# Attention over channels and a feed-forward layer in one kernel: the first pair of chunks by eight plain products, sums of the first weights later, other places for the first loads

## The chip, the cores and the metric

The kernel runs on one core of a Trainium2 chip. The metric is the device time of one execution in microseconds (us); of the kernel before there are three runs. One further execution was recorded by the profiler. Its page calls the engines PE (matrix engine; PEld is its loading of the stationary operand), DVE (vector engine), ACT (scalar engine), POOL and SP (which issues the transfers).

## The reference

For each of 4 batches with N = 6080 tokens and C = 256 channels, k and q are normalised along the tokens, a 256 x 256 score matrix of channel against channel goes through a softmax, and v is multiplied by it. The result goes through a feed-forward layer of width 2048 with the exact gelu.

```
qn = q / (norm(q, axis=1) + 1e-06);  kn = k / (norm(k, axis=1) + 1e-06)
s = kn.transpose(0, 2, 1) @ qn / tau
a = exp(s - s.max(-1));  a /= a.sum(-1) + 1e-09
x = (v @ a).reshape(B * N, C)
h = x @ w_in
out = (0.5 * h * (1 + erf(h / sqrt(2)))) @ w_out
```

The feed-forward weights come as float64.

## The kernel before, in words

The attention matrix is folded into the first weights. For each batch the kernel computes a @ w_in (256 x 2048, in four groups of 512 columns, `w_group`), so that tokens go straight from v to h. All large products are done in three passes on pairs (high, low) of a rounded value and its remainder: high x high, high x low, low x high.

**Opening.** `load_first` loads 24 tiles of 512 KB with q and k of batch 0, then the first four of batch 1 (`FILL`), 13 tiles ahead (`AHEAD`). `qk_first` adds each tile to the scores. The squares for the norms come from two sources: for the first `NSQ` tiles from the tiles themselves (`squares`: a square on ACT, an add on DVE), for the rest from a transposed copy of q and k in pieces of 512 KB (`norm_part`, squares with a sum on ACT). Between the tiles there are loads of v for the first pair (`load_v`, 1 MB) and of the first units of raw weights. `qk_fill` gives PE score matmuls of batch 1 during the softmax of batch 0.

**Narrowing.** The float64 weights are turned into high and low parts on the chip, 16 units of 512 columns: `narrow` is eight DVE operations and two on ACT, in an order where most wait for the one before. Units "in" feed `w_group`, units "out" feed the second products. `load_w` puts a raw unit in one of three buffers (`raw`), so the load of a later unit waits until an earlier one is narrowed; two of the units use buffers of their own (`raw_w`). `NARROWS` says behind which score tiles a unit is narrowed, `paces` how many behind each step of the first pair. The narrowed parts are also stored to DRAM (`keep`), from where later pairs load them.

**Main part.** Tokens are taken in pairs of chunks of up to 512 (`PAIRS`, six per batch) and hidden columns in eight units of 256 (`NU`), so a step is (batch, pair, unit). `first_products` computes the 2 x 2 blocks of h with Strassen's seven products (Winograd's form), 21 matmuls. It needs sums of the weight blocks (S1 to S4) and of the v blocks (T1 to T4), copies three partial results on ACT (L461) and adds on DVE (L466), then takes gelu twice on ACT (L449 and L450) and its remainder on DVE (L451). `second_products`, 24 matmuls (L511 to L513), runs one step behind, interleaved with the first products of the next step. `extras` issues what lies beside a step: the next weight group at the first pair's units 0, 2 and 4, loads, sums for the next pair. `w_group` has 12 matmuls (L362 to L364), and the weights' sums and splits follow it at once; for the very first group they are taken in the order in which the products need them (`w_split`).

**Order.** Dependencies are tracked by tile. A planner places the instructions on each engine by its own estimates of times, with a priority by the order of the text; the softmax and the first weight group have a higher one. On the chip each engine then keeps that order, so a PE matmul at the head of the queue whose input is late holds up what stands behind it. Buffers are shared by name: a new tile of a name waits until the old one's last reader is done.

```
ORDER = ((A11, B11), (S1, T1), (S2, T2), (A12, B21), (S3, T3), (S4, B22), (A22, T4))
```

Of the kernel before, what the change touches and what calls it, by code (L numbers as in the profile page):

```python
# [10 lines left out]
F32R = mybir.dt.float32r  # L11
U32 = mybir.dt.uint32
# [4 lines left out]
P = 128  # L17
# [22 lines left out]
NSJ = NS // (JS * P)  # L40
NSC = NJ * P // NS

NSQ = 4 * NSJ

NARROWS = (4, 7, 12, 18, 20)

GAPS = (7, 4, 2)

# [2 lines left out]

A11, A22, A12, S1, S2, S3, S4 = range(7)
B11, B21, B22, T1, T2, T3, T4 = range(7)


@with_exitstack
def channel_attention_gelu_ffn(ctx, tc, qk, kqt, vt, tau, w_in, w_out, out):
# [30 lines left out]
    def f32(ap):  # L88
        return ap.bitcast(F32)
# [117 lines left out]

    def load_w(src):

        if len(units) in (11, 12):  # L210
            raw = pst.tile([P, src.shape[-1], 2], U32, name="raw_w", bufs=2)
        else:
            raw = pqk.tile([P, src.shape[-1], 2], U32, name="raw", bufs=3)
        nc.sync.dma_start(out=raw, in_=src.bitcast(U32).rearrange("p (n w) -> p n w", w=2))
        return raw

# [126 lines left out]
        state["e"], state["rden"] = (eh, el), rden  # L343


    def w_split(g, i, src):
        nc.scalar.copy(out=whs[g][:, i], in_=src)
        nc.vector.tensor_tensor(out=wls[g][:, i], in0=src, in1=f32(whs[g][:, i]), op=ALU.subtract)  # L348

    def w_group(b, g):  # L350

        eh, el = state["e"]
        win = wins.pop((b, g))
        first = (b, g) == (0, 0)
        tmp = pqk.tile([P, 8, 2, P], F32, name="hl")
        a21, a11, a22, a12 = (tmp[:, i] for i in range(4))
        s1, s2, s3, s4 = (tmp[:, 4 + i] for i in range(4))
        for m in range(NCT):
            cs = slice(m * P, (m + 1) * P)
            pwt = bank()  # L360
            for d in range(NCT):
                nc.tensor.matmul(pwt, eh[:, d, cs], win[:, 0, d], start=(d == 0), stop=False)  # L362
                nc.tensor.matmul(pwt, eh[:, d, cs], win[:, 1, d], start=False, stop=False)
                nc.tensor.matmul(pwt, el[:, d, cs], win[:, 0, d], start=False, stop=(d == NCT - 1))  # L364
            nc.scalar.activation(out=tmp[:, 2 * m:2 * m + 2], in_=pwt.rearrange("p (q r c) -> p r q c", q=2, r=2),
                                 func=AF.Copy, scale=state["rden"][:, m:m + 1])
            if first and m == 0:
                w_split(g, A11, a11)
        tt = nc.vector.tensor_tensor
        if first:  # L370

            tt(out=s1, in0=a21, in1=a22, op=ALU.add)
            w_split(g, S1, s1)
            tt(out=s2, in0=s1, in1=a11, op=ALU.subtract)
            w_split(g, S2, s2)
            w_split(g, A12, a12)
            tt(out=s3, in0=a11, in1=a21, op=ALU.subtract)
            w_split(g, S3, s3)
            tt(out=s4, in0=a12, in1=s2, op=ALU.subtract)
            w_split(g, S4, s4)  # L380
            w_split(g, A22, a22)
            return
        tt(out=s1, in0=a21, in1=a22, op=ALU.add)
        tt(out=s3, in0=a11, in1=a21, op=ALU.subtract)
        tt(out=s2, in0=s1, in1=a11, op=ALU.subtract)
        tt(out=s4, in0=a12, in1=s2, op=ALU.subtract)
        for to, of in ((slice(0, 3), slice(1, 4)), (slice(3, 7), slice(4, 8))):
            (nc.scalar.copy if b == 0 else nc.vector.tensor_copy)(out=whs[g][:, to], in_=tmp[:, of])
            tt(out=wls[g][:, to], in0=tmp[:, of], in1=f32(whs[g][:, to]), op=ALU.subtract)


# [2 lines left out]
    def load_v(b, p):  # L394
        t0, n = PAIRS[p]
        raw = pv.tile([P, NCT, 2 * NT], F32, name="v_raw")
        nc.sync.dma_start(out=raw[:, :, :2 * n],
                          in_=vt[:, b * N + t0:b * N + t0 + 2 * n].rearrange("(t p) n -> p t n", p=P))
        vraw[b, p] = raw
# [20 lines left out]
    def v_split(b, p, i):  # L420
        n = PAIRS[p][1]
        x = v_blocks(b, p)
        src = {B11: x[0, 0], B21: x[1, 0], B22: x[1, 1]}.get(i)
        if src is None:
            src = vts[b, p][i - T1][:, :n]
        hi = pv.tile([P, NT], F32R, name=f"vh{i}")
        lo = pv.tile([P, NT], F32R, name=f"vl{i}")
        nc.scalar.copy(out=hi[:, :n], in_=src)
        nc.vector.tensor_tensor(out=lo[:, :n], in0=src, in1=f32(hi[:, :n]), op=ALU.subtract)
        vops[b, p, i] = hi, lo  # L430
# [23 lines left out]
    def first_products(b, p, u):  # L454
# [38 lines left out]
        do(6, one, False, True)  # L493
        out[0, 0] = gelu(one[:, :n], n)

    po = {}

    def second_products(b, p, u, blocks):
# [32 lines left out]
    def load_unit():  # L531
        kind, g, d = units.pop(0)
        src = w_in64[:, d, g * NT:(g + 1) * NT] if kind == "in" else w_out64[:, g * 2 * C:(g + 1) * 2 * C]
        loaded.append((kind, g, d, load_w(src)))
# [28 lines left out]
             ("in", 2, 0), ("in", 2, 1), ("out", 2, 0), ("out", 3, 0), ("in", 3, 0), ("in", 3, 1), ("out", 4, 0),  # L563
             ("out", 5, 0), ("out", 6, 0), ("out", 7, 0)]

    paces = (1, 2, 1, 2, 2, 1, 1)
    loaded = deque()


    pieces = [(t, c) for c in range(NSQ // NSJ, NSC) for t in range(2 * NCT)]  # L570
    for i in range(AHEAD):
        load_first(i)
        if i in (1, 3, 9):
            load_unit()
        if i in (5, 8, 11):
            norm_part(0, *pieces.pop(0))
        if i == 7:
            load_v(0, 0)
    nc.sync.dma_start(out=taut, in_=tau)
    nc.vector.reciprocal(out=rtau, in_=taut)  # L580
    for js in range(NQS):
        qk_first(js)
        if js + AHEAD < NQS + FILL:
            load_first(js + AHEAD)
            if js % 2 == 1 and pieces:
                norm_part(0, *pieces.pop(0))
        elif len(units) > 11:
            load_unit()
        if js in NARROWS:
            narrow_unit()  # L590
        if js in (10, 11):
            v_sums(0, 0, js - 10)
        if 12 <= js < 19:
            v_split(0, 0, ORDER[js - 12][1])
    for x in held:
        keep(*x)
    fill = qk_fill()
# [29 lines left out]
    def extras(b, p, u):  # L627

        w = p * NU + u
        nxt = (b, p, u + 3)  # L630
        if nxt[2] >= NU:
            nxt = (b, p + 1, nxt[2] - NU)
        if nxt[1] == NP:
            nxt = (b + 1, 0, nxt[2])
        if nxt[0] < B and nxt[:2] != (0, 0):
            load_wo(nxt)
        if (b, p) == (0, 0):
            if u % 2 == 0 and u // 2 + 1 < NWG:
                w_group(0, u // 2 + 1)
        if b > 0 and w == 1:  # L640
            w_group(b, NWG - 1)
        pair = (b, p + 1) if p + 1 < NP else (b + 1, 0)
        if pair[0] < B:
            if u == 1:
                load_v(*pair)
            if u in (4, 5):
                v_sums(*pair, u - 4)
        if b + 1 == B:
            return
        start, num, den = (8, 5, 2) if b == 0 else (2, 3, 1)  # L650
        for k in range(FILL // NB if b == 0 else 0, NQS // NB):
            at = start + k * num // den
            if w == at:
                for m in range(NCT):
                    burst(b + 1, k, m)
                for t in range(NB):
                    hls.pop((b + 1, k * NB + t))
            before = start + (k - 1) * num // den
            if w == (before + 1 if k else at - 1):
                for t in range(NB):  # L660
                    split_qk(b + 1, k * NB + t)
            if w == (before if k else at - 2):
                for t in range(NB):
                    load_qk(b + 1, k * NB + t)
        n0 = 8
        if n0 <= w < n0 + 2 * NCT * NSC:
            with behind("kept"):
                norm_part(b + 1, *divmod(w - n0, NSC))
        if w == 37:
            state["stages"] = softmax(False, ps_h, "ph")  # L670
        if w >= 37:
            next(state["stages"], None)
        if w in (40, 42, 44, 46):
            load_win(b + 1, (w - 40) // 2)
        if w in (42, 44, 46):
            w_group(b + 1, (w - 42) // 2)
# [2 lines left out]
    second = iter(())  # L679
    for b, p, u in steps:  # L680
        pair = (b, p + 1) if p + 1 < NP else (b + 1, 0)
        for i, _ in enumerate(first_products(b, p, u)):
            next(second, None)
            if u == NU - 1 and pair[0] < B:
                v_split(*pair, ORDER[i][1])
        if u == NU - 1 and pair[0] < B:
            v_split(*pair, ORDER[6][1])
        for _ in second:
            pass
        if (b, p) == (0, 0):  # L690
            for _ in range(paces[u] if u < len(paces) else 0):
                narrow_unit()
                if units:
                    load_unit()
        extras(b, p, u)
        second = second_products(b, p, u, state.pop("blocks"))
# [30 lines left out]
```

## Time and profile before

| | |
|---|---|
| time, median of 3 runs | 2208.83 us (2208.10 to 2211.41) |
| span of the profiled execution (its own time) | 2207.9 us |
| PE busy | 2179.6 us (99%) |
| DVE busy | 1402.2 us (64%) |
| ACT busy | 1444.0 us (65%) |
| DMA, mean over the span | 122 GB/s |

A busy share is an average over stages. The opening lasts to about 55 us, softmax and first weights to about 69, the first pair to about 180; there other engines are fuller than the average. In rows of instructions the figures are start (or none, in groups), time, engine, line of the kernel, operation, written tile <- read tiles, shape and count; what stands in brackets is idle time of the engine before the instruction, and what ended it.

### The profile page before, as it was taken

Reading aid. Unit: us, or ns where it says so; the run is one execution under the profiler, and the core shown is the slowest. Engines: PE = TensorE matmul, PEld = TensorE weight load, DVE = VectorE, ACT = ScalarE, POOL = GpSimd, SP = SyncE. Lnnn points to the kernel's source line nnn. Section 1 sums busy time; section 2 is a strip of 40 time slices with the busy share of each in tenths; the row PEclk is TensorE's granted clock in tenths of the full one; section 3 lists DMA queues with packets and bytes.
Section 4 is the critical chain, followed back from the end, with each engine's and each line's share of the span. In section 5 each row is a group of like instructions: output and inputs, shape, how many; then the busy total and the mean of one; then the engine's idle time right before and its main releaser. Section 6 shows DMA issues by size and latency. Waiting matters only on the chain.

```text
span 2207.9 us, 26235 instructions
## 1 busy us (share of the span) xinstructions
PE 2179.6 (99%) x9640; PEld 1787.3 (81%) x9640; DVE 1402.2 (64%) x2205; ACT 1444.0 (65%) x2625; POOL 1.3 (0%) x8
## 2 busy tenths in 40 slices
PE   8899999999999999999999999999999999999999
PEld 6678777888888888888888888888888888888888
DVE  6896757565576665756667657567466555554554
ACT  6678887557875565665766656656576666666665
POOL 0000000000000000000000000000000000000000
PEclk9999999999999999999999999999999999999999
DMA  9557775232652332322224223232122122222221
GB/s 377 196 170 253 243 238 190 78 112 89 235 192 84 125 105 86 109 93 91 89 103 143 98 85 124 67 124 95 48 105 93 59 89 71 70 87 69 73 76 48
DMA packets 77632, 269.61 MB, mean 122 GB/s; under 512 B 7744, under 2 KB 9792, under 8 KB 75456
## 3 DMA queue, kind: packets, MB, share of 16 engines
q1 hardware_dynamic: 77504, 267.94, 35.7%
q8 instruction: 76, 1.25, 0.2%
q14 instruction: 52, 0.43, 0.1%
HBM read 234.62 MB, written 33.29 MB: 121 GB/s over the span
## 4 chain that ended last, share of the span: by engine, by line
PE 87%; ACT 5%; DMA 4%; DVE 3%; issue 1%; SPq 0%; ACTq 0%; DVEq 0%
PE po L513 15%; PE po L511 14%; PE po L512 14%; PE ph L443 13%; PE ph L441 13%; PE ph L442 13%; DMA kqc<-kqt 3%; PE ph L187 2%; ACT kqc L205 2%; PE ph L189 1%; ACT gh L449 1%; ACT g L450 1%; DVE acc L135 1%; DMA raw<-qk 1%; DMA v_raw<-vt 1%
## 5 line engine op out<-in xcount | busy, mean ns | idle before, releaser
L451 DVE TENSOR_TENSOR gl<-g,gh 128x512 fp32r<-128x512 f32 (+1 forms) x768 | 522.6, 682 | 158.1 <-ACT g L450 155.9
L513 PE MATMUL po<-gh,wo 128*128 128x512 f32 (+1 forms) x1536 | 604.7, 394 | 0.0
L511 PE MATMUL po<-gh,wo 128*128 128x512 f32 (+1 forms) x1536 | 597.4, 390 | 0.0
L512 PE MATMUL po<-gl,wo 128*128 128x512 f32 (+1 forms) x1536 | 596.2, 388 | 0.5 <-DVE gl L451 0.5
L466 DVE TENSOR_TENSOR h<-ph,p 128x512 f32<-128x512 f32 (+1 forms) x384 | 262.5, 684 | 520.0 <-PE ph L443 406.1
L449 ACT ACTIVATE gh<-h 128x512 fp32r<-128x512 f32 (+1 forms) x576 | 360.9, 627 | 288.2 <-DVE h L466 284.5
L441 PE MATMUL ph<-vh,wh 128*128 128x512 f32 (+1 forms) x1344 | 526.1, 392 | 9.4 <-ACT p L461 4.0
L443 PE MATMUL ph<-vh,wl 128*128 128x512 f32 (+1 forms) x1344 | 526.5, 392 | 0.0
L442 PE MATMUL ph<-vl,wh 128*128 128x512 f32 (+1 forms) x1344 | 525.5, 391 | 0.0
L461 ACT COPY p<-ph 128x512 f32<-128x512 f32 (+1 forms) x384 | 221.9, 583 | 249.4 <-PE ph L443 249.1
L450 ACT ACTIVATE g<-h 128x512 f32<-128x512 f32 (+1 forms) x576 | 352.7, 612 | 0.0
L512 PEld LDWEIGHTS po<-gl,wo 128*128 128x128 f32 x1536 | 288.5, 188 | 64.9 <-DVE gl L451 1.2
L511 PEld LDWEIGHTS po<-gh,wo 128*128 128x128 f32 x1536 | 288.2, 188 | 62.4 <-ACT gh L449 1.5
L513 PEld LDWEIGHTS po<-gh,wo 128*128 128x128 f32 x1536 | 288.4, 188 | 61.5
L441 PEld LDWEIGHTS ph<-vh,wh 128*128 128x128 f32 x1344 | 252.9, 188 | 71.0 <-ACT p L461 8.4
L442 PEld LDWEIGHTS ph<-vl,wh 128*128 128x128 f32 x1344 | 253.2, 188 | 55.9
L443 PEld LDWEIGHTS ph<-vh,wl 128*128 128x128 f32 x1344 | 253.0, 188 | 51.8 <-DVE wl L348 0.2
L461 ACT COPY u<-ph 128x512 f32<-128x512 f32 (+1 forms) x192 | 111.7, 582 | 113.6 <-PE ph L443 113.5
L466 DVE TENSOR_TENSOR h<-ph,u 128x512 f32<-128x512 f32 (+1 forms) x192 | 131.1, 683 | 3.3
L450 ACT ACTIVATE g<-ph 128x512 f32<-128x512 f32 (+1 forms) x192 | 112.0, 583 | 0.0
L449 ACT ACTIVATE gh<-ph 128x512 fp32r<-128x512 f32 (+1 forms) x192 | 110.4, 575 | 0.0
L187 PE MATMUL ph<-hl 128*128 128x512 f32 x272 | 96.0, 392 | 0.0
(131 smaller groups left out, 1309.8 us busy)
## 6 DMA issues: line engine op xcount, KB each, us to landing
wo<-keep_out SPq DMA_DIRECT2D x184, 512.0 KB, 3.3
raw<-qk SPq DMA_DIRECT2D x95, 512.0 KB, 4.4
kqc<-kqt SPq DMA_DIRECT2D x72, 512.0 KB, 4.4
v_raw<-vt SPq DMA_DIRECT2D x20, 1024.0 KB, 5.2
out<-osb SPq DMA_DIRECT2D x40, 512.0 KB, 3.2
win<-keep_in SPq DMA_DIRECT2D x12, 1024.0 KB, 4.8
kq<-kqt SPq DMA_DIRECT2D x8, 512.0 KB, 9.0
raw<-w_out SPq DMA_DIRECT2D x8, 512.0 KB, 3.8
```

The costliest lines, as they stand in the source:

```text
L187: nc.tensor.matmul(s, hl[:, 0, j, 0, cs], hl[:, :, j, 1], start=(i == 0), stop=False, skip_group_check=True)
L441: nc.tensor.matmul(ps[:, :n], wh, hi[:, :n], start=start, stop=False, skip_group_check=True)
L442: nc.tensor.matmul(ps[:, :n], wh, lo[:, :n], start=False, stop=False, skip_group_check=True)
L443: nc.tensor.matmul(ps[:, :n], wl, hi[:, :n], start=False, stop=stop, skip_group_check=True)
L449: nc.scalar.activation(out=gh[:, :n], in_=src, func=AF.Gelu)
L450: nc.scalar.activation(out=g[:, :n], in_=src, func=AF.Gelu)
L451: nc.vector.tensor_tensor(out=gl[:, :n], in0=g[:, :n], in1=f32(gh[:, :n]), op=ALU.subtract)
L461: nc.scalar.copy(out=t[:, :n], in_=ps[:, :n])
L466: nc.vector.tensor_tensor(out=h[:, :n], in0=ps[:, :n], in1=t[:, :n], op=ALU.add)
L511: nc.tensor.matmul(o, wo[:, 0, i, cs], gh[:, :n], start=first, stop=False)
L512: nc.tensor.matmul(o, wo[:, 0, i, cs], gl[:, :n], start=False, stop=False)
L513: nc.tensor.matmul(o, wo[:, 1, i, cs], gh[:, :n], start=False, stop=last)
```

## The change

1. The first pair of chunks of the first batch is done by `plain_products`: four blocks of h, each the sum of two products in PSUM, 24 matmuls per unit in place of 21. No copies and no adds follow; gelu reads PSUM. Of v it needs the blocks B11, B21, B12, B22 and no sums; B12 uses T1's buffers. Of the weights it needs A11, A12, A21, A22 and no sums; A21 lies in buffers of T2 and T3.
2. In the first batch `w_group` splits these four blocks in `w_first`. The sums S1 to S4 and their splits, first used by the second pair, are in `w_sums`, called at units 0, 2, 4, 6 of the first pair.
3. `NSQ` goes from 16 to 20 tiles, so four norm pieces are left instead of eight.
4. Places of the first loads: weight units behind tiles 3, 10 and 27 (1, 3 and 9 before), norm pieces behind 7, 14, 17 and 20, v behind 25 (7 before). Two units are narrowed in the opening, behind tiles 12 and 18, in place of five; each step of the first pair narrows two. The buffers `raw_w` go.

As `plain_products` yields seven times, the last operand of the next pair is split twice in the last unit.

```
-NSQ = 4 * NSJ
-NARROWS = (4, 7, 12, 18, 20)
+NSQ = 5 * NSJ
+EXTRAS = {3: 'w', 7: 'n', 10: 'w', 14: 'n', 17: 'n', 20: 'n', 25: 'v', 27: 'w'}
+NARROWS = (12, 18)
...
+    def w_both(hi, lo, src):
+        nc.scalar.copy(out=hi, in_=src)
+        nc.vector.tensor_tensor(out=lo, in0=src, in1=f32(hi), op=ALU.subtract)
+    def w_first(g, m, tmp):
+        if m == 0:
+            name = (f"vh{T2}", f"vl{T2}", f"vh{T3}", f"vl{T3}")[g]
+            a21s[g] = pv.tile([P, 2, 2, P], F32R, name=name)
+            w_both(whs[g][:, A11], wls[g][:, A11], tmp[:, 1])
+            w_both(a21s[g][:, 0], a21s[g][:, 1], tmp[:, 0])
+        else:
+            w_both(whs[g][:, A12], wls[g][:, A12], tmp[:, 3])
+            w_both(whs[g][:, A22], wls[g][:, A22], tmp[:, 2])
+    def w_sums(g):
+        tmp = wtmp.pop(g)
+        a21, a11, a22, a12, s1, s2, s3, s4 = (tmp[:, i] for i in range(8))
+        tt = nc.vector.tensor_tensor
+        tt(out=s1, in0=a21, in1=a22, op=ALU.add)
+        tt(out=s3, in0=a11, in1=a21, op=ALU.subtract)
+        tt(out=s2, in0=s1, in1=a11, op=ALU.subtract)
+        tt(out=s4, in0=a12, in1=s2, op=ALU.subtract)
+        w_both(whs[g][:, S1:], wls[g][:, S1:], tmp[:, 4:])
...
+    def plain_products(b, p, u):
...
+        rows = {1: ((wh[:, A11, q], wl[:, A11, q]), (wh[:, A12, q], wl[:, A12, q])),
+                0: ((a21[:, 0, q], a21[:, 1, q]), (wh[:, A22, q], wl[:, A22, q]))}
+        cols = {0: (B11, B21), 1: (B12, B22)}
+        for j in range(2):
+            for i in (1, 0):
+                ps = bank()
+                for k in range(2):
+                    ah, al = rows[i][k]
+                    hi, lo = vops[b, p, cols[j][k]]
+                    for t, (x, y) in enumerate(((ah, hi), (ah, lo), (al, hi))):
+                        nc.tensor.matmul(ps[:, :n], x, y[:, :n], start=(k == 0 and t == 0),
+                                         stop=(k == 1 and t == 2), skip_group_check=True)
+                    if k == 0:
+                        yield
+                out[i, j] = gelu(ps[:, :n], n)
+                if (i, j) != (0, 1):
+                    yield
...
-    paces = (1, 2, 1, 2, 2, 1, 1)
+    paces = (2, 2, 2, 2, 2, 2, 1)
...
+            if u % 2 == 0:
+                w_sums(u // 2)
...
-        for i, _ in enumerate(first_products(b, p, u)):
+        plain = (b, p) == (0, 0)
+        for i, _ in enumerate((plain_products if plain else first_products)(b, p, u)):
```

More of the change, by code (lines that the diff above doesn't have):

```diff
@@ L53 @@
 B11, B21, B22, T1, T2, T3, T4 = range(7)
+B12 = T1
 @with_exitstack
@@ L208, in load_w @@
     def load_w(src):
[L210 to L213, printed above, removed]
+        raw = pqk.tile([P, src.shape[-1], 2], U32, name="raw", bufs=3)
         nc.sync.dma_start(out=raw, in_=src.bitcast(U32).rearrange("p (n w) -> p n w", w=2))
@@ L343, in softmax @@
         state["e"], state["rden"] = (eh, el), rden
-    def w_split(g, i, src):
-        nc.scalar.copy(out=whs[g][:, i], in_=src)
-        nc.vector.tensor_tensor(out=wls[g][:, i], in0=src, in1=f32(whs[g][:, i]), op=ALU.subtract)
+    a21s = {}
+    def w_both(hi, lo, src):
[19 more added lines that the diff above has]
+        w_both(whs[g][:, S1:], wls[g][:, S1:], tmp[:, 4:])
+    wtmp = {}
     def w_group(b, g):
@@ L353, in w_group @@
         win = wins.pop((b, g))
-        first = (b, g) == (0, 0)
         tmp = pqk.tile([P, 8, 2, P], F32, name="hl")
@@ L366, in w_group @@
                                  func=AF.Copy, scale=state["rden"][:, m:m + 1])
-            if first and m == 0:
-                w_split(g, A11, a11)
-        tt = nc.vector.tensor_tensor
[L370 to L382, printed above, removed]
+            if b == 0:
+                w_first(g, m, tmp)
+        if b == 0:
+            wtmp[g] = tmp
+            return
+        tt = nc.vector.tensor_tensor
         tt(out=s1, in0=a21, in1=a22, op=ALU.add)
@@ L387, in w_group @@
         for to, of in ((slice(0, 3), slice(1, 4)), (slice(3, 7), slice(4, 8))):
-            (nc.scalar.copy if b == 0 else nc.vector.tensor_copy)(out=whs[g][:, to], in_=tmp[:, of])
+            nc.vector.tensor_copy(out=whs[g][:, to], in_=tmp[:, of])
             tt(out=wls[g][:, to], in0=tmp[:, of], in1=f32(whs[g][:, to]), op=ALU.subtract)
@@ L423, in v_split @@
         src = {B11: x[0, 0], B21: x[1, 0], B22: x[1, 1]}.get(i)
+        if (b, p) == (0, 0) and i == B12:
+            src = x[0, 1]
         if src is None:
@@ L494, in first_products @@
         out[0, 0] = gelu(one[:, :n], n)
+    def plain_products(b, p, u):
+        n = PAIRS[p][1]
+        g, q = divmod(u, 2)
+        out = state["blocks"] = {}
+        wh, wl = whs[g], wls[g]
+        a21 = a21s[g]
+        rows = {1: ((wh[:, A11, q], wl[:, A11, q]), (wh[:, A12, q], wl[:, A12, q])),
[15 more added lines that the diff above has]
+                    yield
     po = {}
@@ L564, in channel_attention_gelu_ffn, with extra @@
              ("out", 5, 0), ("out", 6, 0), ("out", 7, 0)]
-    paces = (1, 2, 1, 2, 2, 1, 1)
+    paces = (2, 2, 2, 2, 2, 2, 1)
     loaded = deque()
     pieces = [(t, c) for c in range(NSQ // NSJ, NSC) for t in range(2 * NCT)]
+    def extra(i):
+        kind = EXTRAS.get(i)
+        if kind == "w":
+            load_unit()
+        elif kind == "n":
+            norm_part(0, *pieces.pop(0))
+        elif kind == "v":
+            load_v(0, 0)
     for i in range(AHEAD):
         load_first(i)
[L573 to L578, printed above, removed]
+        extra(i)
     nc.sync.dma_start(out=taut, in_=tau)
@@ L584, in channel_attention_gelu_ffn @@
             load_first(js + AHEAD)
-            if js % 2 == 1 and pieces:
-                norm_part(0, *pieces.pop(0))
+            extra(js + AHEAD)
         elif len(units) > 11:
@@ L590, in channel_attention_gelu_ffn @@
             narrow_unit()
[L591 to L594, printed above, removed]
+    for i in (B11, B21, B12, B22):
+        v_split(0, 0, i)
     for x in held:
```

## The prediction

> **What bounds the kernel now.** I read the page first, then windows of busy time, then what TensorE (PE) waited for, then the order of time around the longest waits.
>
> ```profile
> span 2207.9 us, 26235 instructions
> PE 2179.6 (99%) x9640; PEld 1787.3 (81%) x9640; DVE 1402.2 (64%) x2205; ACT 1444.0 (65%) x2625; POOL 1.3 (0%) x8
> ```
>
> The windows (length, then busy time and instructions of PE, PEld, DVE, ACT, POOL, then granted clock, DMA share, GB/s; DVE is VectorE, ACT is ScalarE):
>
> ```profile
> 46.00:62.50 16.50, 16.36 (x83) 13.80 (x83) 4.12 (x16) 6.35 (x14) 0.00 (x0) 1.00 1.02 397
> 62.50:176.00 113.50, 103.36 (x424) 79.20 (x424) 109.47 (x207) 80.97 (x152) 0.00 (x0) 0.97 0.49 171
> 68.58:176.00 107.42, 98.35 (x400) 75.33 (x401) 103.77 (x193) 75.34 (x141) 0.00 (x0) 0.97 0.46 158
> 88.00:118.00 30.00, 30.00 (x131) 24.11 (x130) 29.32 (x55) 21.74 (x39) 0.00 (x0) 1.00 0.34 119
> 140.00:176.00 36.00, 36.00 (x154) 28.36 (x155) 35.51 (x63) 27.40 (x52) 0.00 (x0) 1.00 0.55 188
> 76.20:83.10 6.90, 5.78 (x13) 4.10 (x14) 5.08 (x11) 4.96 (x9) 0.00 (x0) 0.51 0.37 152
> ```
>
> PE is busy for 99% of the span, so what counts is matmuls issued and time in which none starts. The change lies in the first 180 us. There, from 62.5 to 176, VectorE is busy 109.47 of 113.5 us: it is the full engine of that stretch, beside PE.
>
> PE's waits (in all, times, longest), first before 56 us, then from 68 to 190:
>
> ```profile
> PE ph L145 <- DMA raw<-qk: 7.7, 6, 3.5
> ```
>
> ```profile
> PE ph L363 <- DVE win L247: 4.2, 4, 2.0
> PE ph L362 <- ACT win L245: 2.1, 1, 2.1
> PE ph L441 <- ACT g L450: 1.3, 1, 1.3
> PE ph L441 <- ACT p L461: 1.2, 1, 1.2
> PE ph L441 <- ACT wh L347: 1.1, 1, 1.1
> PE ph L441 <- DVE h L466: 0.3, 1, 0.3
> ```
>
> And PE's pace in a full stretch:
>
> ```profile
> 101.40 0.39 PE L511 MATMUL po<-gh,wo 128*128 128x512 f32 x1
> ...
> 104.88 0.40 PE L513 MATMUL po<-gh,wo 128*128 128x512 f32 x1
> ```
>
> Sixteen matmuls start from 101.40 to 104.88, so one costs 3.48/15 = 0.232 us. Then 400 matmuls from 68.58 to 176 need 92.8 us and PE lost 107.4 - 92.8 = 14.6 us there. Saturated VectorE alone is not the loss: from 140 to 176 it is busy 35.51 of 36 and PE's 154 matmuls (35.7 us) fill the window; from 88 to 118 likewise. The loss sits where a matmul of the next weight group (L362, L363) stands at the head of PE's queue and its weights are still being narrowed:
>
> ```profile
> 68.58 0.50 PE L441 MATMUL ph<-vh,wh 128*128 128x512 f32 x1 [1.07 <-ACT wh L347]
> ...
> 70.83 0.40 PE L362 MATMUL ph<-win,eh 128*128 128x512 f32 x1
> 72.03 0.50 PE L363 MATMUL ph<-win,eh 128*128 128x512 f32 x1 [0.81 <-DVE win L247]
> 72.36 0.40 PE L364 MATMUL ph<-win,el 128*128 128x512 f32 x1
> 74.82 0.50 PE L362 MATMUL ph<-win,eh 128*128 128x512 f32 x1 [2.06 <-ACT win L245]
> 77.31 0.80 PE L363 MATMUL ph<-win,eh 128*128 128x512 f32 x1 [1.99 <-DVE win L247]
> ```
>
> and right after it, from 76.2 to 83.1, the granted clock is 0.51. The 13 matmuls there would take 3.0 us at the full pace; of the other 3.9, some 1.2 is the end of the last wait, so the slow clock cost about 2.7.
>
> **The change, part by part.** *First loads.* PE's matmuls on a tile of q and k are pitched like this, and loads follow each other on SP so:
>
> ```profile
> 8.34 1.99 PE L145 MATMUL ph<-raw 128*128 128x256 f32 x8 [1.01 <-DMA raw<-qk]
> ...
> 28.83 26.26 PE L145 MATMUL ph<-raw 128*128 128x256 f32 x112 [0.57 <-DMA raw<-qk]
> ```
>
> ```profile
> 12.16 0.34 SPq L119 DMA_DIRECT2D raw<-qk  x1
> 13.44 0.33 SPq L204 DMA_DIRECT2D kq<-kqt  x1
> ```
>
> The 112 matmuls of 14 tiles take 26.26 us, 1.88 a tile; a 512 KB load takes 13.44 - 12.16 = 1.28 us. Up to the last tile the queue now carries 24 tiles, 3 weight units, 8 norm pieces and v (two loads' worth): 37 x 1.28 = 47.4 us, more than PE's 24 x 1.88 = 45.1. After the change it is 24 tiles, 2 units and 4 pieces: 38.4. So the waits behind the first tile (7.7 - 3.5 = 4.2 us) have no cause; bounds 0 and 4.2, and I take 3.8, since the second tile (1.01) is early in the ramp. V moves from behind the 8th tile to behind the 26th: it is in after 34 loads, some 45 us, and its first use is the first product, now at 68.58; that gap is its cover. Four squares and four adds replace four squares over norm pieces; the adds, of 128x1024 (1.22 us each, L389 below), fall in VectorE's idle time, 12.4 of the 16.5 us from 46 to 62.5. Without that cover the last add would put 1.2 on the path.
>
> *Products.* A unit of the first pair goes from 21 to 24 matmuls: 8 x 3 x 0.232 = **+5.6 us** on PE, nothing hides it. The Trainium skill, page "TensorE: Matmul & The Clock Gate", section "Back-to-back issue gap", gives about 131 ns sustained for 512 columns; by it this term would be 3.1 us and the forecast 2.5 us lower. The row has 232 ns and decides. In return each unit sheds three copies on ScalarE and three adds on VectorE.
>
> ```profile
> 121.44 0.68 DVE L466 TENSOR_TENSOR h<-ph,u 128x512 f32<-128x512 f32 x1
> 122.04 0.68 DVE L451 TENSOR_TENSOR gl<-g,gh 128x512 fp32r<-128x512 f32 x1
> ```
>
> ```profile
> 126.05 0.42 DVE L235 TENSOR_SCALAR kqc<-raw 128x512 uint32<-128x512 uint32 x1
> 126.39 0.69 DVE L239 SCALAR_TENSOR_TENSOR kqc<-kqc,raw 128x512 f32<-128x512 f32 x1
> ```
>
> ```profile
> L389 DVE TENSOR_TENSOR wl<-hl,wh 128x1024 fp32r<-128x1024 f32 x3 | 3.7, 1218 | 0.0
> L389 DVE TENSOR_TENSOR wl<-hl,wh 128x768 fp32r<-128x768 f32 x3 | 2.8, 948 | 0.0
> ```
>
> ```profile
> L384 DVE TENSOR_TENSOR hl<-hl 128x256 f32<-128x256 f32 x3 | 1.3, 417 | 0.0
> ```
>
> In these pairs of rows, and the groups by shape, starts are 0.60 apart for a two-input 128x512 operation and 0.34 for a one-input one; a 128x256 sum lasts 0.42 and also gives 0.34. VectorE sheds 24 x 0.60 = 14.4 us.
>
> *Weights and narrowing.* One narrowing is three of 0.34 and five of 0.60 on VectorE: 4.0 us. Three leave the opening, but two of those (the raw_w ones) ran after 62.5 already, so the stretch gains one: +4.0. A weight group now takes eight 128x256 operations and one of 128x1024 (3.9 us) against four, one of 768 and one of 1024 (3.4): +0.5 for three groups. The last split of the next pair's operands is issued twice: +0.6. VectorE's need becomes 109.5 - 14.4 + 4.0 + 1.5 + 0.6 = 101.2 us. ScalarE, 81 of 113.5 now, loses 24 copies and gains less than that: no bound.
>
> Both engines then come out level. PE starts products at 68.58 - 3.8 = 64.8 and needs 424 x 0.232 = 98.4: 163.2. VectorE starts at 58.7 and needs 101.2 plus the 4.0 it idles today: 163.9, less what it narrows earlier. It can, because the raw weights come sooner:
>
> ```profile
> L214 SPq DMA_DIRECT2D raw_w<-w_in x2: 327/328/328, 49.3 to 50.5; - x2
> ```
>
> ```profile
> DMA to landing us min/median/max: 10.4/10.9/11.4
> ```
>
> ```profile
> SPq L544 <- DVE win L247: 21.6, 3, 18.7
> ```
>
> Those two landed at about 60 and 62; after the change units 3 to 5 are loads 37 to 39, at 37 to 39 x 1.28 us and the start of the queue, about 48 to 52. The last row is SP standing for 18.7 us at a store that waits for a narrowing, with later loads behind it; that wait shortens with the narrowing, and whoever needs those loads (the second step's narrowing) has a unit of slack. POOL is passed by nothing.
>
> So PE's 14.6 lost microseconds can fall to nothing or stay, and with three narrowings ahead of the second group they could grow; bounds 0 and 18. I take 4.5, nearer the two level windows, since the second group is now wanted only after 48 matmuls (11 us), while PE has first products without Strassen adds to run: **-10.1**. What is late next: the narrowing of the second group once (about 2) and the w_out unit that a step's second products need at once (about 1), and restarts.
>
> *Softmax.* Units 3 to 5 now land inside the softmax chain, whose short operations hand over to VectorE some five times; each may find a 0.60 us narrowing in front: 0 to 3.0, taken as **+0.6**, because before the change VectorE narrows there only at its end. *Border.* The next pair's second operand can be split only when the last but one k-step of the last unit has read its slot: about 1.3 us of ScalarE and VectorE beside 24 second products (5.6 us): 0, or 0.7 without them. The first weights, written in another order, 0 (the wait of 1.1 for L347 stays; it lies before 68.58).
>
> Sum: -3.8 + 5.6 - 10.1 + 0.6 = **-7.7**. The profiled span of 2207.9 becomes 2200.2; the median of the three runs is 0.9 above that span, 2208.83, so **2201.1**.
>
> **Rivals.** With X for PE's loss in the stretch, the change is X - 12.2.
>
> 1. *No wait is left.* For it: the levels 163.2 and 163.9 and 12 us of idle VectorE in which to narrow early. Against: the order on PE is fixed beforehand, and today's shows it misjudged. X about 1: -11.2, 2197.6.
> 2. *The waits move but stay, and the clock falls again.* X from 8 to 16, say 10.5: -1.7, 2207. For it: two of every unit's narrowings still end just ahead of what uses them. The clock fell after waits of 0.81, 2.06 and 1.99 us, so one such cluster brings back 2.7. The Trainium skill, same page, section "Why this matters for your kernels", asks only that no gap pass about 3 us. By that rule such waits would keep the clock, and this rival would cost 2.7 less; the 0.51 in the window row speaks against the rule.
> 3. *Slower: narrowing holds PE at each group.* If no narrowing runs early, VectorE has three of them, the group's splits (1.4) and two copies (1.2) from 58.7: done at 73.3, while PE ends the first unit at 70.4. If PE's order has the group next, it waits 2.9, and a slow clock adds 2.7. The same at all three groups is X = 16.8, and with restarts 18: +5.8, 2214.6. It decides from 5.5 us per group upward. Against: 48 matmuls may stand before the group.
>
> **How the numbers follow.** Forecast 0.50 (own range 2198 to 2204.5, X from 2 to 8), no wait left 0.16, waits stay 0.22, slower 0.12. Within 0.2%, 4.4 us, is about what a measurement here cannot tell from no change: the first two cases are faster (0.66), the third the same (0.22), the fourth slower (0.12). The range 2196 to 2211 leaves out the slower case and the tip of the first rival.
>
> **What the profile after would show.** Opening: PE's waits on tiles near 3.5 to 4 in all, the last score matmul near 51 instead of 55. First stretch: L466 and L461 start only in the second pair, VectorE below 96% busy, PE's row L363 <- L247 under 3, the clock at 1.0 after 8 us. Softmax: first product 13.5 us behind the last score matmul, or up to 3 more. The prediction is wrong if PE stands at a group matmul for more than 5 us, if the slow clock returns, or if the opening still waits for tiles.

## The result

| | median | runs |
|---|---|---|
| before | 2209.11 us | 4, 2208.10 to 2211.41 |
| changed | 2194.51 us | 4, 2192.47 to 2201.28 |

The ratio is 0.9935 (95% interval 0.9918 to 0.9952): about 14.6 us faster, nearly twice the forecast of 7.7. Measured again beside other kernels (below), the changed kernel took 2197.25 us against 2211.17, 13.9 us less, ratio 0.9938 (0.9926 to 0.9949). Each experiment's ratio is to executions of the kernel before that ran beside it, without one of 2690 us in a slow state, and need not equal the quotient of two medians given here.

The page of the changed kernel, then two windows of it and one of the kernel before (length, then busy time and instructions of PE, PEld, DVE, ACT, POOL, granted clock, DMA share, GB/s):

```profile
span 2192.7 us, 26257 instructions
PE 2180.0 (99%) x9664; PEld 1792.8 (82%) x9664; DVE 1391.5 (63%) x2186; ACT 1432.3 (65%) x2602; POOL 1.3 (0%) x8
```

```profile
64.00:160.00 96.00, 95.37 (x409) 75.72 (x408) 95.15 (x184) 65.93 (x125) 0.00 (x0) 1.00 0.57 191
```

```profile
64.00:259.20 195.20, 194.55 (x841) 155.07 (x840) 161.86 (x289) 153.87 (x291) 0.00 (x0) 1.00 0.66 220
```

```profile
68.60:272.10 203.50, 193.70 (x818) 152.33 (x819) 167.80 (x287) 156.62 (x295) 0.00 (x0) 0.98 0.60 203
```

PE's busy time is the same in both pages; it starts 24 more matmuls in a span 15.2 us shorter. In the first pair VectorE (DVE) is still full, 95.15 of 96 us, but PE is full beside it: 409 matmuls start there, and at 0.2305 us, the pace of an undisturbed stretch, they need 94.3 of 96 us. The last two rows are the first two pairs, from the first product to VectorE's last copy of the second pair's output: 195.2 us against 203.5, with the 24 matmuls more in it. The clock is back at 1.00.

What PE waited for in the changed kernel, before 56 us and from 60 to 180:

```profile
PE ph L149 <- DMA raw<-qk: 4.6, 2, 3.7
```

```profile
PE po L555 <- DVE gl L469: 0.6, 1, 0.6
PE ph L388 <- ACT eh L340: 0.2, 1, 0.2
```

The 10 us of waits of the first pair are down to one of 0.6. The next weight group still meets an unfinished narrowing, but the planner has put products between its matmuls:

```profile
74.70 0.63 PE L388 MATMUL ph<-win,eh 128*128 128x512 f32 x2
75.17 0.39 PE L531 MATMUL ph<-vh,wh 128*128 128x512 f32 x1
...
77.47 0.39 PE L531 MATMUL ph<-vl,wh 128*128 128x512 f32 x1
77.70 0.40 PE L389 MATMUL ph<-win,eh 128*128 128x512 f32 x1
```

L388 takes the high part of the narrowed weights, L389 needs the low part; where PE stood idle before the change, eleven product matmuls run.

The same account for all kernels, from the traces of one execution each. The second column is the end of the last score matmul, in us from the start. "Loss" adds up, over matmul starts more than 0.30 us apart, what exceeds 0.2305 us. "Rest" is the span behind the second pair. e0 to e11 are the experiments.

| kernel | last score matmul | from there to the first product | first two pairs | PE loss there | rest |
|---|---|---|---|---|---|
| before | 55.1 | 13.5 | 203.5 | 16.3 | 1935.8 |
| changed | 50.5 | 13.5 | 195.2 | 3.1 | 1933.5 |
| changed again, e0 | 48.3 | 13.5 | 195.1 | 3.0 | 1938.6 |
| e1 rest of the change alone | 50.5 | 13.9 | 213.3 | 26.0 | 1940.3 |
| e2 products alone | 55.0 | 13.5 | 195.8 | 5.0 | 1936.7 |
| e3 sums at once | 48.2 | 13.5 | 200.7 | 9.0 | 1933.1 |
| e4 fourth pass | 48.1 | 13.5 | 210.1 | 3.7 | 1937.9 |
| e5 adds put back | 48.1 | 13.5 | 208.8 | 16.5 | 1933.3 |
| e6 group later (on before) | 55.3 | 13.5 | 202.3 | 16.0 | 1936.1 |
| e7 20 warming matmuls | 49.4 | 13.5 | 195.2 | 3.1 | 1937.9 |
| e8 five narrowed early | 49.7 | 13.5 | 206.5 | 13.5 | 1934.0 |
| e9 six warming matmuls | 48.8 | 13.5 | 194.7 | 3.1 | 1937.0 |
| e10 narrowing on POOL | 48.3 | 13.9 | 225.5 | 39.4 | 1938.1 |
| e11 three matmuls less | 48.3 | 13.5 | 197.0 | 11.0 | 1931.8 |

"Rest" runs over 8.5 us, and e0, which is the changed kernel again, lies above the kernel before in it; so the 2.3 us of the 15.2 between the two spans that lie in it are not put down to the change.

### The profile page after: what moved, and what is told of

The parts are those of the page before. It is cut to its first block, busy times and chain, and to the rows that moved or that the text cites. A ratio compares the mean times of both kernels' runs of the same rounds, so it can differ in the third digit from the quotient of the medians.

```text
span 2192.7 us, 26257 instructions
## 1 busy us (share of the span) xinstructions
PE 2180.0 (99%) x9664; PEld 1792.8 (82%) x9664; DVE 1391.5 (63%) x2186; ACT 1432.3 (65%) x2602; POOL 1.3 (0%) x8
## 4 chain that ended last, share of the span: by engine, by line
PE 89%; ACT 5%; DMA 5%; DVE 1%; issue 0%; SPq 0%; ACTq 0%; DVEq 0%
PE po L556 15%; PE po L554 14%; PE po L555 14%; PE ph L461 12%; PE ph L460 12%; PE ph L459 12%; DMA kqc<-kqt 4%; PE ph L191 3%; ACT kqc L209 2%; PE ph L149 2%; PE ph L531 2%; PE ph L193 1%; ACT gh L467 1%; ACT g L468 1%; PE ph L390 1%; PE ph L388 1%
## 5 line engine op out<-in xcount | busy, mean ns | idle before, releaser
L484 DVE TENSOR_TENSOR h<-ph,p 128x512 f32<-128x512 f32 (+1 forms) x368 | 251.6, 684 | 518.8 <-PE ph L461 411.8
L467 ACT ACTIVATE gh<-h 128x512 fp32r<-128x512 f32 (+1 forms) x552 | 345.8, 626 | 283.1 <-DVE h L484 280.8
L459 PE MATMUL ph<-vh,wh 128*128 128x512 f32 (+1 forms) x1288 | 502.8, 391 | 3.0 <-ACT p L479 1.6
L461 PE MATMUL ph<-vh,wl 128*128 128x512 f32 (+1 forms) x1288 | 503.7, 391 | 0.0
L460 PE MATMUL ph<-vl,wh 128*128 128x512 f32 (+1 forms) x1288 | 502.7, 390 | 0.0
L468 ACT ACTIVATE g<-h 128x512 f32<-128x512 f32 (+1 forms) x552 | 337.7, 612 | 0.0
L460 PEld LDWEIGHTS ph<-vl,wh 128*128 128x128 f32 x1288 | 242.1, 188 | 54.0
L461 PEld LDWEIGHTS ph<-vh,wl 128*128 128x128 f32 x1288 | 241.9, 188 | 49.1
L467 ACT ACTIVATE gh<-ph 128x512 fp32r<-128x512 f32 (+1 forms) x216 | 125.1, 580 | 13.0 <-PE po L556 8.3
L468 ACT ACTIVATE g<-ph 128x512 f32<-128x512 f32 (+1 forms) x216 | 126.5, 587 | 0.3 <-DVE gl L469 0.3
```

What stands on the lines that cost most here:

```text
L459: nc.tensor.matmul(ps[:, :n], wh, hi[:, :n], start=start, stop=False, skip_group_check=True)
L460: nc.tensor.matmul(ps[:, :n], wh, lo[:, :n], start=False, stop=False, skip_group_check=True)
L461: nc.tensor.matmul(ps[:, :n], wl, hi[:, :n], start=False, stop=stop, skip_group_check=True)
L467: nc.scalar.activation(out=gh[:, :n], in_=src, func=AF.Gelu)
L468: nc.scalar.activation(out=g[:, :n], in_=src, func=AF.Gelu)
L484: nc.vector.tensor_tensor(out=h[:, :n], in0=ps[:, :n], in1=t[:, :n], op=ALU.add)
```

## The experiments

The theory after the result: VectorE set the pace of the first pair, and the change pays in matmuls for 24 adds taken from it. The rival: the same gain came from other places of loads and narrowings, and the products only cost.

**e1, the rest of the change without the products.** The kernel before with the new loads, `NSQ`, `NARROWS` and `paces`; v's sums and its seven splits behind the score tiles.

```
-            if js % 2 == 1 and pieces:
-                norm_part(0, *pieces.pop(0))
+            extra(js + AHEAD)
...
-    paces = (1, 2, 1, 2, 2, 1, 1)
+    paces = (2, 2, 2, 2, 2, 2, 1)
```

> Everything of the change but the plain products: first loads, five tiles' worth of squares, two narrowings in the opening and two per step; the first pair stays with Strassen's products, adds and early weight sums. Theory A (the waits of the first pair went because VectorE sheds 24 adds and no product waits for an add): the opening gives its 4.6 us, the loss of 14.8 us in the first pair stays and grows by the narrowing that moved there (4.0): about 2208, PE loss in the first pair 15 to 20 us. Theory B (they went because narrowings and loads stand elsewhere): the loss falls to 2 or 3 us without the 24 matmuls: about 2191.

2215.82 us, ratio 1.0036 (1.0023 to 1.0049): slower than before. The opening gave its 4.6 us, the first two pairs lost 9.8. The rival falls. The theory's numbers were missed too: about 2208 was expected, and PE's loss in the first pair was 22.8 us, not 15 to 20.

**e2, the products without the rest.** The changed kernel with the loads, norm pieces and narrowings of the opening as before.

```
-    for i in (B11, B21, B12, B22):
-        v_split(0, 0, i)
+        if 12 <= js < 16:
+            v_split(0, 0, (B11, B21, B12, B22)[js - 12])
```

> Plain products and deferred sums alone; loads, norm pieces and narrowings of the opening as in the kernel before. Theory A: first pair gains 13.2 and pays 5.6, opening unchanged (last score matmul at 55): about -7.6 of before, 2201. Theory B: pays 5.6 and keeps most of the loss: 2212 to 2215.

2202.95 us, ratio 0.9972 (0.9962 to 0.9982): about 6 us faster, first two pairs 7.7 us shorter (the theory said 7.6), opening unchanged. The parts do not add up: +6 alone and -6 alone, -14 together. Moving narrowings into the first pair costs 10 us while VectorE is over-full there, and next to nothing once it isn't.

**e5, the load put back without the dependencies.** Three adds per unit on VectorE that nothing reads.

```
+                if (i, j) != (0, 0):
+                    gh, gl = out[i, j]
+                    h = pg.tile([P, NT], F32, name="h", bufs=2)
+                    nc.vector.tensor_tensor(out=h[:, :n], in0=f32(gh)[:, :n], in1=f32(gl)[:, :n], op=ALU.add)
```

> The changed kernel with three adds of 128x512 per unit put back on VectorE, 24 in all (14.4 us); nothing reads them and no PE matmul waits for one. Theory A1 (what helped is VectorE's load): VectorE, busy 95 of 96 us already, needs 14 us more, PE waits again, first pair 10 to 14 us longer: 2204 to 2208. Theory A2 (what helped is that no product and no gelu waits for an add or a weight sum, so VectorE's backlog lies where PE has other work): 0 to 4 us, 2194 to 2198.

2208.24 us, ratio 0.9990 (0.9980 to 1.0001): the gain is gone. PE's waits from 50 to 180 us, three longest rows, and the first 96 us of products:

```profile
PE ph L389 <- DVE win L248: 4.2, 2, 2.2
PE po L560 <- DVE wo L248: 2.2, 3, 0.9
PE ph L459 <- ACT p L479: 1.4, 1, 1.4
```

```profile
61.70:157.70 96.00, 87.98 (x364) 68.10 (x363) 94.16 (x181) 58.42 (x109) 0.00 (x0) 0.98 0.49 166
```

14.4 us more of VectorE make the first two pairs 13.7 us longer than in e0, although no matmul waits for an add: PE starts 364 matmuls in 96 us and not 409. The wait at the group's narrowing is back at the same place (L389 for L248, 4.2 us in all). More load on VectorE is enough to bring the loss back; no matmul has to depend on the adds. ScalarE kept its relief of 24 copies here, so the copies are not what paid. The planner ordered this kernel anew, and how much of the 13.7 us is order was not separated.

**e6, the place of the wait.** The kernel before, weight groups one unit later.

```
-            if u % 2 == 0 and u // 2 + 1 < NWG:
+            if u % 2 == 1 and u // 2 + 1 < NWG:
```

> The kernel before, with the next weight group issued at the first pair's units 1, 3 and 5 and not 0, 2 and 4; nothing else. If the first pair loses its 14.8 us because a group's matmul stands at the head of PE's queue too early, the three waits for L247 (4.2) and the one for L245 (2.1) go, with them the slow clock (2.7): 9 us less, 2201. If VectorE's load sets the stretch, the wait only moves to other matmuls: within 2 us of before, 2208 to 2213.

2209.75 us, ratio 0.9994 (0.9984 to 1.0003). No matmul of a group waits for a narrowing any more; there is one wait of 6.9 us on a copy instead. The copy stood on ScalarE behind two operations of narrowings that waited for VectorE:

```profile
71.45 0.40 PE L443 MATMUL ph<-vh,wl 128*128 128x512 f32 x1
78.71 0.80 PE L441 MATMUL ph<-vh,wh 128*128 128x512 f32 x1 [6.86 <-ACT p L461]
```

```profile
74.32 0.62 ACT L245 CAST win<-nt 128x512 fp32r<-128x512 f32 x1 [2.67 <-DVE nt L239]
77.52 0.67 ACT L232 ACTIVATE kqc<-raw 128x512 f32<-128x512 f32 x1 [2.58 <-DVE win L247]
78.10 1.04 ACT L461 COPY p<-ph 128x512 f32<-128x512 f32 x2
```

So the matmul at the head of the queue showed where PE waits, not why.

**e4 and e11, PE's side.** A fourth pass in each product; and three matmuls less per unit, which leaves out half of one block of h.

```
-((ah, hi), (ah, lo), (al, hi))
+((ah, hi), (ah, lo), (al, hi), (al, lo))
```

```
-                for k in range(2):
+                last = 0 if (i, j) == (0, 1) else 1
+                for k in range(last + 1):
```

> The changed kernel with a fourth pass (low x low) in each plain product: 8 more matmuls a unit, 64 in all, no other work. If PE is the bound of the first pair, each costs its full 0.2305 us: +14.8, 2209. If VectorE (95 of 96 us busy) sets the pace there, PE has room and it costs less than 5 us: below 2200.

> The changed kernel with three matmuls of each unit of the first pair left out (the second half of one of the four sums, so that one block of h lacks it): 21 matmuls a unit as with Strassen's products, but no adds and no copies; VectorE and ScalarE have the same work as in the changed kernel. If PE alone sets the first pair, all 24 come back, 5.6 us: ratio to before lower by 0.0025 than the changed kernel's 0.9938. If VectorE, 95 of 96 us busy, is as full as PE, PE's saving turns into waits: first pair less than 2 us shorter, its loss 5 us and more.

e4: 2208.19 us, ratio 0.9988 (0.9979 to 0.9998); the first two pairs are 15.1 us longer than in e0 for 64 matmuls, 0.236 each, full price. e11: 2194.59 us, ratio 0.9929 (0.9915 to 0.9942), within the uncertainty of the changed kernel; the first two pairs took 197.0 us, not less than e0's 195.1, and PE's loss rose from 3.0 to 11.0 (in the first pair alone from 1.6 to 5.7). Its first 96 us:

```profile
61.80:157.80 96.00, 92.87 (x392) 72.31 (x391) 95.59 (x185) 66.93 (x126) 0.00 (x0) 1.00 0.56 192
```

VectorE is busy 95 us as before, PE starts 17 matmuls fewer than in e0 and waits. The changed kernel stands where both engines are full: more work on PE costs in full, less gives nothing.

**e3, the place of the sums.** `w_sums(g)` at once in `w_group`.

```
+            w_sums(g)
...
-            if u % 2 == 0:
-                w_sums(u // 2)
```

> The changed kernel with the four sums and their splits right behind each weight group, not behind the step. If the place of the sums matters (they stand ahead of narrowings on VectorE, 2.5 us each time), PE's loss in the first pair grows by 2.5 to 8 us: 2197 to 2202. If VectorE has that slack anyway, as PE waited only 1.6 us there: within 1 us of the changed kernel, 2194 to 2195.

2199.01 us, ratio 0.9954 (0.9941 to 0.9967). The interval overlaps the changed kernel's, so the time settles nothing; in the trace the first two pairs are 5.6 us longer than in e0 and PE loses 6 us more there. VectorE has the same work here, so its place costs as well: with VectorE full, work that nobody needs yet delays work that somebody does.

**e8, early narrowing.** Five narrowings in the opening again.

```
-NARROWS = (12, 18)
+NARROWS = (12, 16, 18, 20, 22)
-    paces = (2, 2, 2, 2, 2, 2, 1)
+    paces = (1, 2, 1, 2, 2, 1, 1)
```

> The changed kernel with five narrowings asked for in the opening again (behind tiles 12, 16, 18, 20, 22) and the old number per step. Three of them can then use VectorE's idle 9 us during the end of the scores and the softmax. If narrowing there disturbs the softmax chain, the first product comes more than 13.5 us behind the last score matmul, by up to 3 us: 2195 to 2198. If not, VectorE is relieved in the first pair, but PE lost only 1.6 us there: 2193 to 2195.

2207.07 us, ratio 0.9986 (0.9976 to 0.9997). Neither expectation held: the softmax chain kept its 13.5 us, and yet PE lost 10.5 us more behind it than in e0. PE's longest wait from 50 to 180 us, and ScalarE's waits from 62 to 80:

```profile
PE po L554 <- ACT gh L467: 7.4, 1, 7.4
```

```profile
ACT win L246 <- DVE nt L240: 5.8, 2, 3.0
ACT kqc L233 <- DVE win L248: 2.9, 1, 2.9
```

The narrowings now stand ahead of the first unit's gelus in ScalarE's order, and each of their casts waits for VectorE; the second products had no input until the third was through, and the clock was at half from 73.0 to 79.8. In the changed kernel the casts stand behind the first gelus.

**e0, e7, e9, the start.** The changed kernel unchanged; with 12 small matmuls ahead of the first tile and 8 behind it; with 6 ahead.

```
+    warm = ps_o.tile([P, NT], F32, name="po")
+    for _ in range(6):
+        nc.tensor.matmul(warm[:, 0:P], ones, ones, start=True, stop=True)
```

> The changed kernel once more, with nothing changed. In the profiles so far the slow clock of the start ended at 7.2, 7.9, 12.3, 12.5 or 13.2 us, and the last score matmul of the kernels with the new loads at 48.1 or 50.5. If that explains the spread, executions fall into two groups about 2.4 us apart, 2192 and 2194.5; and PE's loss behind the second pair, 6.4 us in the changed kernel's profile against 9.1 before, is seen again between 5 and 9.

> The changed kernel with 12 small matmuls on a constant before the first tile's matmuls and 8 behind them, so that PE is not idle at the start; their result is not used. If the slow clock of the start ends because PE was active for some microseconds, it now ends by 8 us every time and the last score matmul is at 48.1: 2192, and 2.4 us less than the slower executions. If its end has another cause, nothing changes: 2194.5. If the tiles are the limit after that, less than 1 us comes of it.

> The changed kernel with 6 small matmuls on a constant ahead of the first tile and none behind it (the 20 of the run before took 5.1 us and 2.0 us and held up both first tiles; its clock was full from 5.7 us). If they end by 3.7 us and the clock is full by 6 or 8 us, the last score matmul is at 48.0 in each execution: 0.3 us under the best and 2.4 under the worst of the changed kernel, median 1 us under it. If PE's activity does not decide, no change.

e7: 2197.85 us, ratio 0.9935 (0.9923 to 0.9947). e9: 2195.74 us, ratio 0.9938 (0.9923 to 0.9952). Neither differs from e0 (0.9938). PE in the changed kernel, in e0 and in e9 (the six small matmuls show as twelve records):

```profile
3.66 3.78 PE L149 MATMUL ph<-raw 128*128 128x256 f32 x8 [3.66 <-DMA raw<-qk]
8.33 42.13 PE L149 MATMUL ph<-raw 128*128 128x256 f32 x184 [0.90 <-DMA raw<-qk]
```

```profile
3.65 3.78 PE L149 MATMUL ph<-raw 128*128 128x256 f32 x8 [3.65 <-DMA raw<-qk]
7.87 40.44 PE L149 MATMUL ph<-raw 128*128 128x256 f32 x184 [0.43 <-DMA raw<-qk]
```

```profile
1.13 2.93 PE L630 MATMUL po<-ones 128*128 128x128 f32 x12 [1.13 <-POOL ones L98]
3.85 2.73 PE L149 MATMUL ph<-raw 128*128 128x256 f32 x8
8.18 19.33 PE L149 MATMUL ph<-raw 128*128 128x256 f32 x88 [1.60 <-DMA raw<-qk]
```

The same 184 matmuls take 42.13 or 40.44 us: in the first execution the slow clock ends at 12.7 us, in e0 at 8.8. Warming makes it end at 5.5, as expected, but then PE stands 1.6 us for the second tile, and the last score matmul is at 48.8, no earlier than in e0. The loads are what PE waits for next, 1.6 us there and 0.24 again at 27.8; warming gains nothing that the times can tell. The two groups of times that were expected of e0 aren't there: 2195.5 to 2199.5 without a gap. PE's loss behind the second pair, expected between 5 and 9 us, was 12.0 there; the clock was at half from 585.7 to 589.1, behind 3.4 us in which PE was busy 0.47.

**e10, relief without matmuls.** e1 with the last two operations of a narrowing on POOL.

```
-        nc.vector.tensor_tensor(out=w, in0=w, in1=f32(hi), op=ALU.subtract)
-        nc.vector.tensor_tensor(out=lo, in0=w, in1=tail, op=ALU.add)
+        nc.gpsimd.tensor_tensor(out=w, in0=w, in1=f32(hi), op=ALU.subtract)
+        nc.gpsimd.tensor_tensor(out=lo, in0=w, in1=tail, op=ALU.add)
```

> Strassen's products in the first pair with all of the rest of the change (the first experiment), and the last two operations of each narrowing (two of eight, 0.60 us each on VectorE) on POOL. If VectorE's load is the cause, 14 narrowings give back 16.8 us of it, and PE's loss in the first pair falls from 22.8 to between 3 and 8 us, without the 24 matmuls: 2194 to 2200. If POOL is much slower than VectorE in these operations, or slows VectorE down beside it, the narrowing is late at every group: 2215 and more.

2227.61 us, ratio 1.0077 (1.0062 to 1.0091). Groups of POOL and of VectorE from 64 to 180 us:

```profile
L245 POOL TENSOR_TENSOR kqc<-kqc,wo 128x512 f32<-128x512 f32 x8 | 14.3, 1786 | 73.1 <-DVE raw L241 43.5 <-ACT wo L244 24.1 <-DVE wl L388 5.5
L246 POOL TENSOR_TENSOR win<-kqc 128x512 fp32r<-128x512 f32 x6 | 8.3, 1388 | 2.2 <-DVE kqc L242 1.5 <-POOL kqc L245 0.7
```

```profile
L242 DVE SCALAR_TENSOR_TENSOR kqc<-raw 128x512 f32<-128x512 uint32 x14 | 15.7, 1124 | 0.0
...
L229 DVE TENSOR_SCALAR raw<-raw 128x512 f32<-128x512 f32 x14 | 8.9, 648 | 0.0
```

POOL takes 1.4 to 1.8 us for what VectorE does in 0.69, and some of VectorE's own operations grow beside it, from 0.69 to 1.12 and from 0.42 to 0.65 (means of e1 and of e10). From 64 to 160 us VectorE is busy 86.15 of 96 and PE starts 270 matmuls: VectorE is no longer full, and yet PE loses 39.4 us in the first two pairs. So load isn't the only thing that can hold PE; that it is the longer narrowing here is argued from the rows, not tested. No kernel here beats the changed one by more than the measurement can tell.

## Why the prediction came out too slow

The direction held and the mechanism in part: VectorE's relief and the opening paid, but the prediction looked for PE's loss in the wrong place. -7.7 was forecast, -14.6 measured. Of the 7.5 us between the forecast and the two spans (-15.2), 3.8 lie in the first two pairs, 0.8 in the opening, 0.6 in the softmax and 2.3 behind the second pair.

- **PE's loss, taken as 4.5 us and -10.1.** This is the step that failed. Over the stretch from the first product to the end of the first pair the loss fell from 14.8 to 1.6 us, by 13.1; 1.6 lies outside the 2 to 8 us of its own range. The text had the right sum just above: PE done at 163.2, VectorE at 163.9, where the kernel before had 176. That alone is -12.1, 2196.7. It then added waits on top, by the reading that "Saturated VectorE alone is not the loss" and that a group matmul at the head of PE's queue is a loss of its own. e6 shows that such a wait moves when the group moves, and e5 that it comes back with VectorE's load alone. It was the place where VectorE's surplus came due.
- **24 matmuls, +5.6 us, "nothing hides it".** Right as a price upward (e4: 0.236 us each), wrong as a term to be forecast apart from the waits: with 21 matmuls (e11) the stretch is no shorter, and what PE saves turns into waits. By the 131 ns of the Trainium skill, page "TensorE: Matmul & The Clock Gate", section "Back-to-back issue gap", e4's 64 matmuls would have cost an estimated 8.4 us; they cost 15.1.
- **VectorE's need, 101.2 us, 8.3 less than before.** Nearly borne out: from 62.5 to 272.1 us VectorE was busy 173.5 us before the change, and 166.4 from 57.9 to 259.2 behind it, 7.1 less. But VectorE is not below 96% busy, as the text expected: from 62.5 to 176 us it is busy 112.19 of 113.5, beyond the end of the first pair.
- **Opening, -3.8.** 4.6 in the profile of the change, 6.8 in e0, up to 7.0 in other kernels with these loads (e4, e5), against bounds of 0 to 4.2. The 1.88 us a tile that was taken for PE's own pace held short waits for loads, too short to be listed as idle time. Without them, in the changed kernel, 150 matmuls take 32.54 us, 1.74 a tile:

```profile
15.77 32.54 PE L149 MATMUL ph<-raw 128*128 128x256 f32 x150
```

  The clock of the start was no help: it was full from 7.95 us before the change, from 12.7 in the profile of the change and from 8.8 in e0, so that the first profile shows the smaller gain.
- **Softmax, +0.6, and narrowing in VectorE's idle time.** 0.0: 13.5 us in both, as no narrowing ran there. SP's loads of the raw units and VectorE in the changed kernel:

```profile
41.63 0.33 SPq L215 DMA_DIRECT2D raw<-w_out  x1
42.95 1.60 SPq L215 DMA_DIRECT2D raw<-w_in  x2
```

```profile
52.18 0.16 DVE L296 TENSOR_TENSOR small<-po,small 128x4 f32<-128x4 f32 x1 [9.12 <-PE po L172]
...
60.56 0.76 DVE L231 TENSOR_SCALAR raw<-raw 128x512 f32<-128x512 f32 x2
```

  The two loads of `w_in` were issued some six microseconds earlier than before (49.3 to 50.5), but the narrowing starts at 60.56, and the 9 us in which VectorE stood idle before 52.18 are not used: in the text it follows the fill, and its scratch buffer (`kqc`) lies in the pool that is opened only when the opening's pool is closed. So the first rival came nearest (2197.6), in part by luck: its two level engines were there, its early narrowing was not.
- **Second rival's clock.** It did not fall in the changed kernel's first pair, but it fell where waits came back (e5, e8, e1), without a gap of 3 us in the first pairs of e1 and e5 (between starts just ahead, at most 1.59 and 2.45); see below.
- **Slower rival.** It did not come. Nearest to it is e8, by another path: narrowings ahead of the first gelus hold PE for 7.4 us, once, and the clock halves. That needs narrowings asked for earlier, not later.

## What to carry to other kernels

Where two engines are full in a stretch, as here, forecast the greater of their two needs first, and don't add the waits of today to it: here the wait at the head of the queue was where the fuller engine's surplus was paid, and it moved when the order did. That sum is a least time: order costs beyond it (e3 5.6 us, e8 11.4). A pace read from a row can hold waits too short to be listed. A dear operation on one engine can be a gain if it takes load from the one that sets the stretch, and the balance is seen by adding dummy load to one side and taking load from the other. Parts of a change that depend on one engine's load can't be priced one by one: here +6 and -6 made -14.

## What the runs showed of the hardware

The granted clock fell to half for 3.4 us or for 6.8 us, each time, between the first matmuls and the last, behind 3.4 us in which PE was busy for little more than half the time or less. No single gap had to be long. e1, the two drops of its first pair and the 3.4 us ahead of each:

```profile
91.70:95.10 3.40, 3.40 (x8) 2.72 (x9) 3.23 (x5) 3.40 (x7) 0.00 (x0) 0.50 0.02 5
88.30:91.70 3.40, 1.91 (x7) 0.79 (x6) 3.40 (x8) 2.87 (x6) 0.00 (x0) 1.00 0.38 157
108.80:112.20 3.40, 3.40 (x10) 2.64 (x9) 3.40 (x7) 1.69 (x4) 0.00 (x0) 0.51 0.01 2
105.40:108.80 3.40, 1.60 (x6) 0.85 (x6) 3.40 (x8) 3.40 (x7) 0.00 (x0) 0.99 0.00 0
```

PE was busy 1.91 and 1.60 of 3.40 us there; its longest gap between starts was 1.27 and 1.59 us. The Trainium skill, page "TensorE: Matmul & The Clock Gate", section "Why this matters for your kernels", warns of gaps above about 3 us; here the clock fell without one. Such a stretch does not always bring a drop. In the same execution PE was busy 0.97 of 3.40 us, and the clock stayed full behind it:

```profile
69.60:73.00 3.40, 0.97 (x3) 0.49 (x3) 3.40 (x7) 2.86 (x6) 0.00 (x0) 1.00 0.00 0
73.00:76.40 3.40, 1.94 (x6) 0.97 (x6) 3.40 (x8) 2.48 (x6) 0.00 (x0) 1.00 0.18 23
```

What decides between the two is open here.

At the start the clock became full between 7.0 (e6) and 13.2 us (e1) in kernels whose first matmul started alike, at 3.5 to 3.7 us; in the opening that was worth up to 2.4 us at the last score matmul (50.5 in the profile of the change, 48.1 in e5). And beside POOL, some of VectorE's operations took up to 1.6 times as long (0.69 us in e1, 1.12 in e10); whether POOL is slowed by VectorE too was not seen.
